# A chunked RWKV-7 recurrence followed by a low-rank mixer: the order of the steps of a slot written out, the block-diagonal state by VectorE, the mixer's u on tokens in place

## The chip, the cores and the metric

The kernel runs on one core of a Trainium2 chip. The metric is the device time of one execution in microseconds (us). Names of engines are those of the profile: PE is TensorE (PEld its weight loads), DVE VectorE, ACT ScalarE, POOL GpSimd, SP the engine that issues the DMAs. "Granted clock" is the share of full speed that TensorE's throttle granted, as the profile records it.

## The reference, cut to what matters

```
for t in range(S):                       # B=4, H=8, S=768, D=40, all float32
    y[t]  = einsum('bhd,bhde->bhe', r[t], state)
    Sa    = einsum('bhde,bhe->bhd', state, a[t])
    state = state * w[t][:, :, None, :] - Sa (x) b[t] + v[t] (x) k[t]
x = y as (B, S, H*D) = (4, 768, 320)
h = (x.T @ U) @ V                        # over the sequence, rank 32
u = x + h.T
out = u + relu(u @ w_ch1) @ w_ch2        # 320 -> 1280 -> 320
```

## The kernel before, in words

**Recurrence.** The sequence is cut into 12 chunks of L = 64 tokens. Two batch entries stand in the two halves of the 128 partitions, so there are 24 units of work (2 pairs of batches by 12 chunks), each with 8 heads. A unit passes through four generators, which `yield` between steps:

- `prep_f` needs only w, a, b: transposes of w and a (`pw`, `pa`), the running product of w by a scan on DVE (`PF`), its transposes `pp` and `pq`, a reciprocal `ip` on DVE, `nBT` on POOL, its transpose `pb`, and the scores `pf`, which go through DRAM (`fd`) into `ln`.
- `substitute` inverts triangular 16 by 16 blocks for two units at a time, in 14 pairs of small products on POOL (tiles `tmp`, `ln`), and stores the result to DRAM (`TD`), from where `fetch` reads it as `tc`.
- `prep_s` joins the blocks (`pg`, `g`, `px`, `t`, `pg2`, `GX`, `px2`), transposes v, r, k (`pv`, `pr`, `pk`) and makes the masked scores `e` and `cm` (from `pe`).
- `carry` is the part that depends on the unit before: `ph` from the state `ST`, `pX`, the outputs `py`, the transpose `pn`, the scores `pg` masked to `ng`, the gains `pd`, the new state `sn`, `sc`, `ST`, and `pS`, transposes of the state for the next unit's `py`. `ST` holds the state of a head pair as a block-diagonal matrix. `XTM` (tokens by 320, in SBUF) takes y.

In slot n stand `carry` of unit n, `prep_s` of unit n + 1, `prep_f` of unit n + 5 and, in every second slot, `substitute`. `merged` takes the step that is next by its share of its generator's steps. A tile framework then places every instruction on its engine's queue and may let it pass others; each engine works through its queue in order. The weights arrive as 64-bit floats in 27 pieces: `piece` loads one into `raw` and converts it to float32 by ACT, four DVE and four POOL instructions, one or two steps a slot.

**Mixer.** After a check of the inputs (`flag`, a branch) the second stage has 6 groups of 4 chunks (512 tokens). `mix(g)` makes `uf`, u transposed (features by tokens), in 3 tiles: transposes of `XTM` and on top of them, in the same PSUM bank, the low-rank part from `V_` and `hut`. `up_proj` makes `hid` in 5 pairs of PSUM banks (`p1`), one of each pair put out by ACT, one by DVE. `down_proj` sums 10 products in a bank, adds the low-rank part again on tokens, adds `XTM` and stores. The mixer's PSUM: 2 banks `p1`, 2 `pu`, 2 `p2`, 2 `ph`.

Of the kernel before, what the change touches and what calls it, by code (L numbers as in the profile page):

```python
# [37 lines left out]
def kernel(  # L38
# [85 lines left out]
    def piece(pool, dst, srcs):  # L124
# [10 lines left out]
        raw = pool.tile([128, WP, 2], I32, name="raw", bufs=2)  # L135
# [30 lines left out]
    with ExitStack() as p1:  # L166
# [106 lines left out]
        def prep_f(u):  # L273
# [17 lines left out]
            square(u, "A", u.nat["A"][:, :, 0:D], 1 / X_HI)  # L291
            yield
            p = one("pp")
# [9 lines left out]
            u.fa = hp.tile([128, NH, L], F32, name="fa")  # L303
            nc.vector.tensor_tensor(out=u.fa[:].rearrange("p h t -> p (h t)"), in0=pa[:], in1=pf[:, 0:NH * L],
                                    op=ALU.mult)
            nc.vector.tensor_copy(u.fa[:, :, 0:1], heads(pa[:])[:, :, 0:1])
            u.fa = u.fa[:].rearrange("p (i x) t -> p i (x t)", x=2)
            u.pe = hp.tile([128, NH, 1], F32, name="pe")
            nc.gpsimd.tensor_copy(u.pe[:], heads(pf[:, 1:])[:, :, L - 1:])
            yield  # L310
            bt = u.nat["BT"]
            nc.gpsimd.tensor_tensor(out=bt[:, :, 0:D], in0=u.nat["B"][:], in1=u.ip[:], op=ALU.mult)  # L312
            square(u, "B", u.nat["B"][:], 1 / X_HI)
            yield
# [3 lines left out]
            fb = qp.tile([128, NP, 128], F32, name="fb", tag="tr", bufs=2)  # L318
# [50 lines left out]
        def prep_s(u):  # L369
# [11 lines left out]
            fv = qp.tile([128, NP, 128], F32, name="fv", tag="tr", bufs=2)  # L381
# [4 lines left out]
            nc.scalar.activation(out=u.fr[:].rearrange("p i t -> p (i t)"), in_=pr[:], func=ACTF.Copy)  # L386
            pk = one("pk")
            up(kt, pk)
            fk = qp.tile([128, NP, 128], F32, name="fk", tag="tr", bufs=2)
            nc.scalar.activation(out=fk[:].rearrange("p i t -> p (i t)"), in_=pk[:], func=ACTF.Copy)  # L390
            square(u, "V", u.nat["V"][:, :, 0:D], 1 / X_HI)
            yield
# [11 lines left out]
            square(u, "R", u.nat["R"][:, :, 0:D], 1 / X_HI)  # L404
            yield
            p = two("pe")
            scores(p, fk, u.fa)
            scores(p, fv, u.fr, NP * DP)
            u.e = qp.tile([128, 2, NP, DP], F32, name="e", bufs=2)

            masked(u.e[:], p[:, :, 0:NP * DP])
            u.cm = qp.tile([128, 2, NP, DP], F32, name="cm", bufs=2)
            masked(u.cm[:], p[:, :, NP * DP:])
            square(u, "K", u.nat["K"][:], 1 / X_HI)
# [129 lines left out]
        def merged(*steps):  # L544

            lists = [[g, 0, n] for g, n in steps]
            while lists:
                x = min(lists, key=lambda x: (x[1] + 0.5) / x[2])
                if next(x[0], x) is x:
                    lists.remove(x)  # L550
                x[1] += 1

        wload = weights(wp)
        units = [Unit(n) for n in range(N)]
        AH = 5
# [235 lines left out]
```

## Time and profile before

| | before |
|---|---|
| median of 3 runs | 1073.66 us (1063.0 to 1081.65) |
| the profiled execution | 1072.85 us, of which the span of its instructions is 1071.0 us |
| PE busy | 903.6 us (84%) |
| DVE, ACT, POOL busy | 330.3, 251.7, 300.4 us |
| granted clock, mean | 0.835 |
| recurrence | first instruction to 707 us; first `XTM` write at 95.5 us, last at 705.2 us |
| mixer | 711.2 us to the end |

A PE matmul row counts records: a float32 matmul leaves two, a transpose one. "[0.80 <-DVE ng]" behind a row is idle time of the engine ahead of it and who ended it. Rows of the windows view give, for each engine, busy us and number of instructions, then the granted clock.

### The profile page before, as it was taken

The numbers are of one execution on the slowest core, as the hardware profiler recorded it, in microseconds if no ns is written. First come the engines' busy times: TensorE is split into PE (matmuls) and PEld (weight loads), VectorE is DVE, ScalarE is ACT, GpSimd is POOL, SyncE is SP. The second block draws the span as 40 slices with busy tenths as digits, with TensorE's granted clock in tenths as the row PEclk, the third lists the DMA queues.
The fourth block names the chain that finished last, engine by engine and source line by source line (L and its number), as shares of the span: only waits on it lengthen the run. The fifth ranks groups of instructions, "written<-read, shape, count | busy, mean of one in ns | idle before, by whom it ended". The sixth has DMA issues, their size and how long they took to land. (4 is left out here: it accounts for less than half of the span.)

```text
span 1071.0 us, 33742 instructions
## 1 busy us (share of the span) xinstructions
PE 903.6 (84%) x15146; PEld 675.0 (63%) x15146; DVE 330.3 (31%) x668; ACT 251.7 (23%) x630; POOL 300.4 (28%) x616
## 2 busy tenths in 40 slices
PE   2558789888788888888997868978989999999988
PEld 2447688777677787776886857853636455454635
DVE  5534334354434445443434214111111110101010
ACT  1223333333433343333333323200000000000010
POOL 5434524453625353525244446000000000000000
PEclk9656777787868787867779668669999999999999
DMA  4464342535252525443525221000000001010001
GB/s 97 70 96 80 50 85 42 95 48 99 45 99 45 96 48 99 70 73 51 94 42 91 51 61 27 3 3 0 13 13 13 12 1 25 1 24 1 22 3 25
DMA packets 262500, 51.19 MB, mean 48 GB/s; under 512 B 256112, under 2 KB 259216, under 8 KB 262352
## 3 DMA queue, kind: packets, MB, share of 16 engines
q1 hardware_dynamic: 262352, 49.01, 26.4%
q8 instruction: 119, 1.95, 0.7%
q14 instruction: 29, 0.24, 0.1%
HBM read 36.11 MB, written 12.86 MB: 46 GB/s over the span
## 5 line engine op out<-in xcount | busy, mean ns | idle before, releaser
L744 PE MATMUL p<-W,hid 128*128 128x320 f32 x480 | 135.8, 438 | 0.0
L729 PE MATMUL p<-uf,W 128*128 128x512 f32 x240 | 111.0, 605 | 16.6 <-ACT hid L734 16.6
L744 PEld LDWEIGHTS p<-W,hid 128*128 128x128 f32 x480 | 89.2, 190 | 45.3 <-issue 11.3
L729 PEld LDWEIGHTS p<-uf,W 128*128 128x128 f32 x240 | 43.1, 189 | 82.3 <-issue 45.8
L734 ACT ACTIVATE hid<-p 128x512 f32<-128x512 f32 x30 | 17.9, 597 | 324.1 <-PE p L732 324.1
L537 PE MATMUL pS<-ID,ST 128*128 128x128 f32 x176 | 43.9, 419 | 35.0 <-POOL ST L523 35.0
L296 DVE RECIPROCAL ip<-pp 128x320 f32<-128x320 f32 x24 | 51.8, 2158 | 46.1 <-PE pp L258 46.0
L735 DVE TENSOR_SCALAR hid<-p 128x512 f32<-128x512 f32 x30 | 20.8, 692 | 139.4 <-PE p L732 139.4
L537 PEld LDWEIGHTS pS<-ID,ST 128*128 128x128 f32 x176 | 35.2, 221 | 37.1 <-POOL ST L523 36.8
L436 PE MATMUL pg<-tt,fm 32*64 32x32 f32 x768 | 43.1, 277 | 13.1 <-DVE tt L428 11.6
L751 DVE TENSOR_TENSOR o<-p,XTM 128x320 f32<-128x320 f32 x24 | 11.8, 492 | 136.8 <-PE p L748 136.8
L436 PEld LDWEIGHTS pg<-tt,fm 32*64 32x64 f32 x768 | 40.0, 203 | 17.5 <-PE px L420 8.1
L156 POOL TENSOR_TENSOR low<-low,unit 128x320 f32<-128x320 f32 (+3 forms) x27 | 22.4, 829 | 100.9 <-ACT low L149 75.9
L350 POOL TENSOR_TENSOR ln<-ln,tmp 128x14 f32<-128x14 f32 (+6 forms) x168 | 45.4, 271 | 11.9
L348 POOL TENSOR_TENSOR tmp<-ln 128x14 f32<-128x14 f32 (+6 forms) x168 | 44.7, 266 | 12.7
L150 DVE TENSOR_SCALAR bits<-raw 128x320 int32<-128x320 int32 (+3 forms) x27 | 17.1, 634 | 96.4 <-DMA raw<-in_moe_w_ch_dram 75.2
L287 DVE COPY seg<-pw 128x8 f32<-128x8 f32 x24 | 4.1, 171 | 132.5 <-PE pw L253 132.5
L523 POOL TENSOR_TENSOR ST<-sc,slot 128x640 f32<-128x640 f32 x22 | 27.6, 1255 | 57.8 <-DVE sc L520 57.8
L446 PEld LDWEIGHTS px<-t,GX 32*64 32x64 f32 x768 | 39.3, 194 | 7.0 <-issue 4.8
L446 PE MATMUL px<-t,GX 32*64 32x32 f32 x768 | 43.7, 271 | 0.0
L312 POOL TENSOR_TENSOR nBT<-nB,ip 128x320 f32<-128x320 f32 x24 | 20.7, 863 | 77.3 <-DVE ip L296 72.4
L463 PE MATMUL ph<-nV,e 64*64 64x40 f32 x768 | 41.1, 282 | 0.0
(155 smaller groups left out, 1660.6 us busy)
## 6 DMA issues: line engine op xcount, KB each, us to landing
fd<-fn SPq DMA_DIRECT2D x48, 128.0 KB, 2.6
raw<-in_moe_w_ch_dram SPq DMA_DIRECT2D x18, 320.0 KB, 4.0
nW<-in_w_dram SPq DMA_DIRECT2D x48, 80.0 KB, 3.1
nA<-in_a_dram SPq DMA_DIRECT2D x48, 80.0 KB, 3.0
nB<-in_b_dram SPq DMA_DIRECT2D x48, 80.0 KB, 2.9
nR<-in_r_dram SPq DMA_DIRECT2D x48, 80.0 KB, 2.8
nK<-in_k_dram SPq DMA_DIRECT2D x48, 80.0 KB, 3.2
nV<-in_v_dram SPq DMA_DIRECT2D x48, 80.0 KB, 3.2
```

Of the source, the lines that this page charges most:

```text
L156: nc.gpsimd.tensor_tensor(out=g, in0=g, in1=e.bitcast(F32), op=ALU.mult)
L296: nc.vector.reciprocal(out=u.ip[:], in_=heads(p[:])[:, :, 0:D])
L348: nc.gpsimd.tensor_tensor(out=x, in0=ln[:, 0:j, j:j + 1].to_broadcast([128, j, n]), in1=ln[:, j:j + 1, j + 1:].to_broadcast([128, j, n]), ...
L350: nc.gpsimd.tensor_tensor(out=ln[:, 0:j, j + 1:], in0=ln[:, 0:j, j + 1:], in1=x, op=ALU.add)
L436: nc.tensor.matmul(out=pg[half(x), 32 * h:32 * h + 32], lhsT=fm[s, h, :], rhs=tt[s, h, :], start=True, stop=True)
L446: nc.tensor.matmul(out=px[half(x), 32 * h:32 * h + 32], lhsT=GX[s, h, :], rhs=t2[s, h, :], start=True, stop=True)
L463: nc.tensor.matmul(out=ph[half(x), s, i], lhsT=u.e[half(x), s, i, :], rhs=vt[half(x), 2 * i + s, 0:D], start=i + s == 0, stop=first, skip_ ...
L523: nc.gpsimd.tensor_tensor(out=ST[:, :, :, 0:D], in0=sc[:].rearrange("p i x e -> p (i x) e").unsqueeze(2).to_broadcast([128, NH, 2, D]), in ...
L537: nc.tensor.transpose(out=p[:, h // 4, 128 * (h % 4):128 * (h % 4 + 1)], in_=ST[:, h].rearrange("p s e -> p (s e)"), identity=ID[:])
L729: nc.tensor.matmul(out=ps_[x][:], lhsT=W1[i][:, (j + x) * 128:(j + x + 1) * 128], rhs=uf[i][:], start=(i == 0), stop=False)
L735: nc.vector.tensor_scalar_max(hid[:, j + 1, :], ps_[1][:], 0.0)
L744: nc.tensor.matmul(out=p[:, 0:DM], lhsT=hid[:, f, 2 * j * L:2 * (j + 1) * L], rhs=W2[:, f, :], start=(f == 0), stop=False, skip_group_chec ...
```

## The change

Five things.

1. `merged` goes; every slot runs the steps in one written order. `prep_f` has five steps instead of six, and its first one runs at the end of the slot before; there is one more slot at the beginning.
2. `ST` is written by DVE, in two `scalar_tensor_tensor` straight from `sn`; `sc` moves from DVE to POOL.
3. `carry` makes `pn` after its first `py`, and the gains are cut in two steps; the squares (a check of input ranges, on ACT) stand at other steps; the tiles `fb`, `fv`, `fk` have 3 buffers for 2.
4. `raw` has 1 buffer for 2, and a piece is loaded and converted within one slot's order.
5. The mixer adds the low-rank part once, on tokens and in place in `XTM` (`mix`), and transposes afterwards (`turn`). `hut` works in four column groups of PE and sums them by a matmul. `p1` has 4 banks, everything else in the mixer shares 2 (`pm`) and 2 (`p2`).

```
-        raw = pool.tile([128, WP, 2], I32, name="raw", bufs=2)
+        raw = pool.tile([128, WP, 2], I32, name="raw")
...
-                state["C"] = sc = qp.tile([128, NP, 2, D], F32, name="sc")
-                nc.vector.tensor_tensor(out=sc[:]..., in0=sn[:]..., in1=u.pe[:].to_broadcast([128, NH, D]), op=ALU.mult)
-                nc.gpsimd.tensor_tensor(out=ST[:, :, :, 0:D], in0=sc[:]..., in1=slot[:]..., op=ALU.mult)
+                sn = sn[:].rearrange("p i x e -> p (i x) e")
+                pe = u.pe[:].to_broadcast([128, NH, D])
+                for s in range(2):
+                    nc.vector.scalar_tensor_tensor(out=ST[:, :, s, 0:D], in0=sn, scalar=slot[:, s:s + 1], in1=pe,
+                                                   op0=ALU.mult, op1=ALU.mult)
+                state["C"] = sc = qp.tile([128, NP, 2, D], F32, name="sc")
+                nc.gpsimd.tensor_tensor(out=sc[:].rearrange("p i x e -> p (i x) e"), in0=sn, in1=pe, op=ALU.mult)
...
+        ORDER = "s c f l s c l c f c l s s l c c f l c s l w f s c l s f s l w"
...
-            merged(*gens)
-            next(wload, None)
-            if n >= 0:
-                next(wload, None)
+            fs = [units[x] if 0 <= x < N else None for x in (n + AH, n + AH + 1)]
+            for key in ORDER.split():
+                g = {"c": c, "s": s, "l": l}.get(key)
+                if key == "f":
+                    nf += 1
+                    x = fs[nf // 5]
+                    g = gen_f(x) if x else None
+                if key == "w" and n >= 1 - AH:
+                    g = wload
+                if g:
+                    next(g, None)
...
+    def hut(pr):
+        hs = mb.tile([128, 2, DM], F32, name="hs", bufs=1)
+        ps_ = [mps.tile([128, 512], F32, name=f"ph{x}", tag="pm", bufs=2) for x in range(2)]
+        for c in range(NCH):
+            for x in range(2):
+                nc.tensor.matmul(out=ps_[x][32 * (c % 4):32 * (c % 4) + 32, 0:DM], lhsT=U_[half(x), c, :],
+                                 rhs=XTM[half(x), pr * NCH + c, :], start=c < 4, stop=c >= NCH - 4,
+                                 skip_group_check=True)
+        nc.vector.tensor_copy(hs[:, 0, :], ps_[0][:, 0:DM])
+        nc.scalar.activation(out=hs[:, 1, :], in_=ps_[1][:, 0:DM], func=ACTF.Copy)
+        huts[pr] = t = mb.tile([RANK, 2, DM], F32, name="hut")
+        for x in range(2):
+            p = mps.tile([128, 512], F32, name="pq", tag="pm", bufs=2)
+            nc.tensor.matmul(out=p[0:RANK, 0:DM], lhsT=IB[:], rhs=hs[:, x, :], start=True, stop=True)
+            nc.vector.tensor_copy(t[:, x, :], p[0:RANK, 0:DM])
...
     def mix(g):
+        for c in range(th * GC, (th + 1) * GC):
+            p = mps.tile([128, 512], F32, name="pv", tag="pm", bufs=2)
+            for x in range(2):
+                nc.tensor.matmul(out=p[half(x), 0:DM], lhsT=V_[:, c * L:(c + 1) * L], rhs=huts[pr][:, x, :],
+                                 start=True, stop=True)
+            x = XTM[:, pr * NCH + c, :]
+            nc.vector.tensor_tensor(out=x, in0=p[:, 0:DM], in1=x, op=ALU.add)
...
-            for x in range(2):
-                nc.tensor.matmul(out=p[:].rearrange("p (j x t) -> p j x t", x=2, t=L)[:, :, x, :],
-                                 lhsT=huts[pr][:, x, 128 * i:128 * i + 128],
-                                 rhs=V_[:, th * GN:(th + 1) * GN], start=False, stop=x == 1,
-                                 skip_group_check=True)
...
-            ps_ = [mps.tile([128, 512], F32, name="p1") for _ in range(2)]
+            ps_ = [mps.tile([128, 512], F32, name="p1", bufs=4) for _ in range(2)]
...
-            for x in range(2):
-                nc.tensor.matmul(out=p[half(x), 0:DM], lhsT=V_[:, c * L:(c + 1) * L], rhs=huts[pr][:, x, 0:DM],
-                                 start=False, stop=True, skip_group_check=True)
...
+        up_proj(hid, uf, (0, 2))
+        if (g + 1) % NT == 0 and g + 1 < NG:
+            hut((g + 1) // NT)
+        up_proj(hid, uf, (4,))
+        if g + 1 < NG:
+            mix(g + 1)
+        up_proj(hid, uf, (6, 8))
+        if g + 1 < NG:
+            uf = turn(g + 1)
         down_proj(g, hid)
```

On PE, the second half of a slot of the recurrence before (from the scores `pg` of `carry` to the next unit's `ph`; L398, L420, L436 and L446 are the four steps that join the blocks in `prep_s`):

```order
L264 MATMUL pg<-fr,xf 64x64 x16
L264 MATMUL pe<-fa,fk 64x64 x16
L509 MATMUL pd<-nV_157,nKT_139 64x40 x16
L528 MATMUL py<-nBT_151,ng 64x40 x8
L398 MATMUL pg<-tt,fm 32x32 x32
L258 MATMUL pn<-ID,xf 128x128 x4
L420 MATMUL px<-tc,g 32x32 x11
L509 MATMUL pd<-nx,nBT_151 64x40 x16
L537 MATMUL pS<-ID,ST 128x128 x2
L436 MATMUL pg_5433<-tt,fm 64x32 x16
L446 MATMUL px_5504<-t_5398,GX 64x32 x6
L463 MATMUL ph<-nV_159,e 64x40 x16
```

The same stretch now (line numbers of the changed kernel: L399, L410, L434, L443 are the four joining steps):

```order
L264 MATMUL pg<-fr,xf 64x64 x16
L507 MATMUL pd<-nV_157,nKT_137 64x40 x16
L507 MATMUL pd<-nx,nBT_145 64x40 x16
L532 MATMUL py<-nBT_145,ng 64x40 x16
L399 MATMUL pg<-tt,fm 32x32 x32
L410 MATMUL px<-tc,g 32x32 x32
L264 MATMUL pf<-fa,fb 64x64 x16
L264 MATMUL pe<-fa,fk 64x64 x16
L541 MATMUL pS<-ID,ST 128x128 x8
L434 MATMUL pg_4102<-tt,fm 64x32 x16
L443 MATMUL px_4136<-t_4020,GX 64x32 x16
L460 MATMUL ph<-nV_159,e 64x40 x16
```

Between each of the four joining steps there now stands other work, the gains stand together, and `pS` stands five groups behind them. (Groups between these that did not change their place, as `pb`, `pw` and `pa`, are left out.)

On DVE, the end of `carry` and the start of the joining before (`tt<-tc` is the transposed block that L398 reads, `g` what L420 reads):

```order
L269 TENSOR_TENSOR ng<-pg,MU 128x512
L269 TENSOR_TENSOR cm<-pe,MU 128x512
L377 STREAM_TRANSPOSE tt<-tc 128x256
L530 SCALAR_TENSOR_TENSOR XTM,SQ<-py,qt 128x320
L402 TENSOR_TENSOR g<-pg,IB 128x256
L518 TENSOR_TENSOR sn<-pd,sc 128x320
L520 TENSOR_TENSOR sc<-sn,pe 128x320
```

And now:

```order
L269 TENSOR_TENSOR ng<-pg,MU 128x512
L521 TENSOR_TENSOR sn<-pd,sc 128x320
L525 SCALAR_TENSOR_TENSOR ST<-sn,slot,pe 128x8x40 x2
L376 STREAM_TRANSPOSE tt<-tc 128x256
L534 SCALAR_TENSOR_TENSOR XTM,SQ<-py,qt 128x320
L403 TENSOR_TENSOR g<-pg,IB 128x256
L418 STREAM_TRANSPOSE tt<-t_4955 128x256
L269 TENSOR_TENSOR e<-pe,MU 128x512
```

The new state and the two writes of `ST` now stand ahead of the transpose `tt<-tc`. Its place differs from slot to slot: of the 23 slots that have it, it is last behind `ST` and `XTM` in 5, behind two of the three in 6, between the two writes of `ST` in 3, directly behind `sn` in 4 and ahead of `ng` in 5.

On PE in the mixer, the end of one group's up projection and what follows before (p_11908 and p_11909 are the last pair of banks):

```order
L732 MATMUL p_11909<-uf_11797,W_2_92 128x512
L707 MATMUL pu<-ID,XTM 128x128 x4
L714 MATMUL pu<-V__89,hut 128x4x64 x2
L711 MATMUL pu<-ID,XTM 64x128 x8
L744 MATMUL p_11949<-W_93,hid 128x320 x10
L748 MATMUL p_11949<-hut,V__89 64x320 x2
```

And now, from the last matmul of the third pair (p_11780, p_11781):

```order
L751 MATMUL p_11781<-uf_11757,W_2_92 128x512
L717 MATMUL pv<-hut,V__89 64x320 x4
L748 MATMUL p_11806<-uf_11739,W_0_90 128x512
L731 MATMUL pu<-ID,XTM 128x128 x8
L762 MATMUL p_11851<-W_93,hid 128x320 x2
L734 MATMUL pu<-ID,XTM 64x128 x8
L762 MATMUL p_11866<-W_93,hid 128x320 x10
```

The low-rank products stand once, inside the up projection, and the transposes alone stand between the two projections.

More of the change, by code (lines that the diff above doesn't have):

```diff
@@ L503, in carry, with gains @@
             yield
[L504 to L511 removed]
+            p = two("pd")
+            def gains(y, z, start):
+                for i in range(NP):
+                    for x, s in ((0, 0), (1, 1), (0, 1), (1, 0)):
+                        nc.tensor.matmul(out=p[half(s), x, D * i:D * (i + 1)], lhsT=y[half(x), 2 * i + s, :],
+                                         rhs=z[half(x), 2 * i + s, 0:D], start=start and i == 0, stop=not start,
+                                         skip_group_check=True)
+            if not last:
+                gains(kt, vt, True)
+            yield
+            if not last:
+                gains(bt, nx, False)
                 dn = p[:, :, 0:NP * D].rearrange("p x (i e) -> p i x e", e=D)
```

127 lines of the change are left out of this document (49 added, 78 removed).

## The prediction

> **What bounds the kernel now.** First the windows view, cut at the first and the 21st write of `XTM` by `carry` and at the start of the mixer (columns: stretch, then busy us and instructions of PE, PEld, DVE, ACT, POOL, granted clock, DMA share, GB/s), with the two timeline rows that set the cuts.
>
> ```profile
> 0.00:95.50 95.50, 48.58 (x812) 41.53 (x812) 44.75 (x102) 26.99 (x70) 42.58 (x118) 0.75 0.51 87
> 95.50:645.40 549.90, 462.24 (x11752) 410.69 (x11753) 220.91 (x452) 191.19 (x495) 240.24 (x481) 0.76 0.40 69
> 645.40:707.00 61.60, 53.83 (x1338) 48.66 (x1336) 17.49 (x40) 15.58 (x35) 17.61 (x18) 0.70 0.04 10
> 711.20:1071.00 359.80, 338.95 (x1248) 174.14 (x1248) 47.03 (x76) 17.92 (x30) 0.00 (x0) 0.99 0.05 11
> 95.53 0.49 DVE L530 SCALAR_TENSOR_TENSOR XTM<-py,qt 128x320 f32<-128x320 f32 x1 [0.51 <-PE py L528]
> 645.39 0.45 DVE L530 SCALAR_TENSOR_TENSOR XTM<-py,qt 128x320 f32<-128x320 f32 x1
> ```
>
> PE carries both stages: 84% busy in the 20 full slots, 94% in the mixer; no other engine passes 44% there. A slot takes 549.9 / 20 = 27.5 us, of which PE idles 87.7 / 20 = 4.4 us. And PE runs at a mean clock of 0.76. Single windows show only 1.00 and 0.50 (a 0.99 is a cut beside the window's edge), so it is at half speed for 48% of the time. Next, who is waited for (PE's waits in these 20 slots: us in total, times, longest), and what the clock does, in windows of 3.4 us.
>
> ```profile
> PE pS L537 <- POOL ST L523: 34.6, 10, 9.1
> PE pd L509 <- DVE ng L269: 12.2, 16, 0.8
> PE pg L436 <- DVE tt L428: 10.6, 10, 1.2
> ```
>
> ```profile
> 284.10:287.50 3.40, 2.13 (x116) 1.84 (x107) 2.99 (x5) 0.00 (x0) 2.34 (x7) 1.00 0.70 109
> 287.50:290.90 3.40, 2.71 (x128) 2.25 (x127) 1.19 (x3) 0.44 (x1) 2.69 (x10) 1.00 0.12 22
> 325.00:328.40 3.40, 3.40 (x28) 3.01 (x30) 0.58 (x2) 1.89 (x7) 1.27 (x1) 0.50 0.00 0
> 328.40:331.80 3.40, 3.40 (x113) 3.15 (x113) 0.00 (x0) 2.73 (x8) 0.59 (x1) 0.99 0.14 25
> 366.00:369.40 3.40, 2.29 (x107) 1.95 (x103) 3.07 (x7) 0.00 (x0) 0.86 (x1) 1.00 0.62 104
> 369.40:372.80 3.40, 3.40 (x112) 2.84 (x112) 0.42 (x1) 0.44 (x1) 0.86 (x1) 0.50 0.65 145
> ```
>
> A window at full clock with 1.27 us idle stayed at 1.00 (first pair), one with 1.11 us idle fell to 0.50 (last pair): about 1.2 us of idle PE in one window is the point where it tips. The middle pair is a return to full clock: that window holds `pb` and `pS`, twelve transposes without a gap. So every short wait is paid twice, once itself and once as a spell at half clock.
>
> What the work of a slot costs at full clock, from the PE timeline:
>
> ```profile
> 303.38 1.93 PE L463 MATMUL ph<-nV,e 64*64 64x40 f32 x32
> 305.24 1.33 PE L468 MATMUL ph<-ST,fa 128*64 128x80 f32 x16
> ...
> 323.69 1.92 PE L436 MATMUL pg<-tt,fm 32*64 32x32 f32 x32 [1.06 <-DVE tt L428]
> ...
> 328.29 0.74 PE L264 MATMUL pf<-fa,fb 64*64 64x64 f32 x32
> 330.01 1.13 PE L463 MATMUL ph<-nV,e 64*64 64x40 f32 x32
> 331.07 0.77 PE L468 MATMUL ph<-ST,fa 128*64 128x80 f32 x16
> 340.14 0.68 PE L509 MATMUL pd<-nV,nKT 64*64 64x40 f32 x32 [0.80 <-DVE ng L269]
> 344.24 0.55 PE L509 MATMUL pd<-nx,nBT 64*64 64x40 f32 x20 [0.68 <-issue]
> 345.21 0.54 PE L528 MATMUL py<-nBT,ng 64*64 64x40 f32 x10
> ```
>
> The same `ph` took 305.24 - 303.38 = 1.86 us at half clock and 331.07 - 330.01 = 1.06 us at full: a factor of 1.75, so a spell at half clock loses 43% of its length. One slot's work runs from L436 at 323.69 to the end of `py` at 345.75: 4.6 us at half clock (to 328.29), worth 2.6 at full, and 17.46 - 0.80 - 0.68 = 16.0 us at full. Together **18.6 us a slot**. The other 27.5 - 18.6 - 4.4 = 4.5 us are the loss to half clock.
>
> **The change, recurrence.** No matmul is removed there, so the 18.6 us stay; what can go are 4.4 us of gaps and 4.5 us of clock.
>
> Gaps that go. `ST` leaves POOL, where it cost 1.26 us in a queue that also holds the block inversion:
>
> ```profile
> L523 POOL TENSOR_TENSOR ST<-sc,slot 128x640 f32<-128x640 f32 x22 | 27.6, 1255 | 57.8 <-DVE sc L520 57.8
> 344.82 0.49 DVE L518 TENSOR_TENSOR sn<-pd,sc 128x320 f32<-128x320 f32 x1 [2.40 <-PE pd L509]
> 345.42 0.49 DVE L520 TENSOR_TENSOR sc<-sn,pe 128x320 f32<-128x320 f32 x1
> 345.83 0.49 DVE L530 SCALAR_TENSOR_TENSOR XTM<-py,qt 128x320 f32<-128x320 f32 x1
> 317.20 0.49 DVE L530 SCALAR_TENSOR_TENSOR XTM<-py,qt 128x320 f32<-128x320 f32 x1 [0.51 <-PE py L528]
> 317.62 0.44 DVE L377 STREAM_TRANSPOSE tt<-tc 128x256 f32<-128x256 f32 x1
> 318.21 1.08 PE L398 MATMUL pg<-tt,fm 32*32 32x32 f32 x64 [1.05 <-DVE tt L377]
> ```
>
> Each of the two new DVE writes is taken at 0.49 us, the row of the same size and kind (`XTM`); bounds are half of it and POOL's 1.26. `pS` now stands five groups (`pb`, `px`, `pf`, twice `pe`) behind the gains, so its 34.6 us go. The gains now have `pk` ahead of them and `ng` is read only by `py` behind them (12.2 us go); the joining steps have `pb`, then `pf`, `pe`, `pS`, then `pw`, `pa` between them (10.6 us and the waits on issue go). `sc` costs POOL about 0.86 us beside PE, less than the 1.26 it gives up. The squares and the third `tr` buffer are costed at nothing: ACT is busy 191 of 550 us; in a slot where a square stands just ahead of `GX` or `nx` it is 0.65 us, which I put into the unforeseen part below.
>
> A gap that stays or grows: L399 (L398 before) waits for `tt<-tc`, which shares DVE with `sn`, the two `ST` and `XTM`. With all four ahead, by the rows: 0.03 to `sn`, 0.60 to the first `ST` (345.42 - 344.82), 0.41 to the second (345.83 - 345.42), 0.41 to `XTM`, 0.42 to the transpose (317.62 - 317.20), 0.44 for it and 0.15 to PE: 2.46 us after the gains. PE has only `py` to do meanwhile, 1.06 us as `ph` of the same shape: **1.40 us idle**. Behind three of them 0.98, between the `ST` 0.57, behind `sn` 0.15, else none. With 5, 6, 3, 4 and 5 such slots that is 15 us; waiting for `g` behind `pb` alone adds some 0.2 us a slot. Sum 0.9 us a slot, and 0.6 for what I cannot foresee: 1.5.
>
> Clock. A 1.40 us gap falls into one window of 3.4 us with at least 1.2 us about 7 times in 10, a 0.98 us gap with the 0.2 of `g` perhaps 3 in 10: 5 x 0.7 + 6 x 0.3 = 5 spells in 23 slots. Each should last until `pf`, `pe`, `pS` have filled a window; before, from L398 at 318.21 to `pf` at 328.29, such a spell took 10 us, about 9 of them work: 4 us lost. That is 21 us; doubled for unforeseen gaps, 1.9 us a slot.
>
> New slot: 18.6 + 1.5 + 1.9 = 22.0 us, **5.5 us less, 110 us over 20 slots**. The last three slots (59.8 us) have fewer steps; at some 15% less, 9 us. The first 95.5 us are left as they are: the same steps of `prep_f` stand there one behind the other. Recurrence: **-119 us**.
>
> Does another engine take over at 22 us? DVE needs 221 / 20 = 11.0 plus 0.5, POOL 12.0, ACT 9.6: on average no. POOL in a slot with the inversion has some 16 us, still less.
>
> The 325.00 row holds mostly transposes, and the clock rose behind it; so I let a spell end at `pS`. The Trainium skill, "TensorE: Matmul & The Clock Gate" ("Part 4: PE-mode transpose"), says instead that a transpose does not count as activity of PE in the same way; by that rule the spells would last past `pS`, about twice as long, and the sum would be 42 us higher, 962. The row does not agree with it.
>
> **The change, mixer.**
>
> ```profile
> PE p L729 <- ACT hid L734: 16.6, 24, 0.8
> 781.36 3.70 PE L729 MATMUL p<-uf,W 128*128 128x512 f32 x8
> 838.23 1.98 PE L729 MATMUL p<-uf,W 128*128 128x512 f32 x4
> L744 PE MATMUL p<-W,hid 128*128 128x320 f32 x480 | 135.8, 438 | 0.0
> L714 PE MATMUL pu<-V__89,hut 32*128 32x256 f32 x72 | 19.7, 397 | 0.0
> L748 PE MATMUL p<-hut,V__89 32*64 32x320 f32 x96 | 18.1, 453 | 0.0
> L695 PE MATMUL ph<-XTM,U__88 64*32 64x320 f32 x96 | 14.7, 464 | 4.3 <-SPq L604 4.3
> ```
>
> A group took 838.23 - 781.36 = 56.9 us, on PE alone and at full clock. Four `p1` banks give PE a free pair while the last is put out: -16.6 us. The low-rank part inside the transposed tiles (L714) goes: -19.7. The one on tokens (L748) only moves, and its 24 adds of 0.49 us lie on DVE, busy 13% there. `hut` is bounded by its 14.7 us and a quarter of that (four column groups). L748, which uses two column groups, took 18.1 / 96 = 0.19 us a record, L744 of the same length 0.28, so I take 9. Its summing matmuls (4 records x 0.28), two copies that PE waits for, and a first `mix` with nothing beside it cost 8 back. Sum: -16.6 - 19.7 - 5.7 + 8 = **-34 us**, between -28 and -40.
>
> **Sum.** 1072.85 - 119 - 34 = 920 us against the profiled execution, which lies 0.8 us under the median of the runs.
>
> **The rivals.**
>
> *The clock holds.* If the gaps are split by the windows' edges, or shorter than worked out, none tips a window: slots of 18.6 + 1.5 = 20.1 us, 148 us less in 20 slots, and 9 + 34: 882 us. The Trainium skill, "TensorE: Matmul & The Clock Gate" ("Why this matters for your kernels"), asks only that no idle gap between matmuls exceeds some 3 us; by that rule no spell would be left and these 882 us would come out. The trace does not agree: at 366.00, 1.11 us in one window was enough.
>
> *A spell in every slot, as before.* If two small gaps meet in most windows, 4.5 us of clock loss stay, with 2.5 us of gaps: slots of 25.6, 38 us less, and 5 + 34: 996 us. For it: a PE that runs faster makes every hand-over to DVE or ACT relatively later.
>
> *The order does not take.* The framework still moves instructions past each other (L399 is written ahead of the gains and stands behind `py`). If the waits only change names, the mixer alone is left: 1039 us.
>
> *Slower: the single `raw` buffer.*
>
> ```profile
> DVE bits L150 <- DMA raw<-in_moe_w_ch_dram: 75.2, 11, 14.7
> raw<-in_moe_w_ch_dram SPq DMA_DIRECT2D x18, 320.0 KB, 4.0
> ```
>
> DVE waited 75.2 / 11 = 6.8 us for `raw` in half of the slots, hidden by its slack. Now L150 stands between `cm` and the scan, with the scan, `fa` and `ip` queued behind it and PE's `pp` behind those, some 1 us of cover. If the load, which can only start when the last conversion has read the buffer, lands 6.8 us late in all 22 slots, that is 22 x (5.8 + 4 of clock) = 216 us on top: 1136 us. It decides from 5 us of lateness a slot. Against it: a load takes 4.0 us to land and now has most of a slot.
>
> **Chances.** Forecast 0.55, clock holds 0.15, a spell in every slot 0.20, order does not take 0.06, slower 0.04. The range 875 to 1000 holds the first three but for their edges. A measurement of this kernel tells about 2% from no change: faster 0.93, same 0.04, slower 0.03.
>
> **What would show it.** Right: mean clock in the slots above 0.85, slots near 22 us, no PE wait for `ST`, the wait for `tt<-tc` the largest left, and about 51 us a mixer group without gaps. Wrong: PE waiting for DVE's scan or for `raw`, a clock still near 0.76, or slots whose idle time exceeds 2 us.

## The result, and the profile after

The changed kernel takes 920.25 us (median of 4 runs, 911.8 to 929.0) against 1073.85 us (median of 4): a ratio of 0.853, 95% interval 0.841 to 0.866. This ratio and those below compare only executions in the faster of two states, for the change those of 911.8 and 914.5 us; medians are of all executions. The profiled execution took 911.8 us, its span 910.1 us at a mean granted clock of 0.902.

The windows view after, cut at the same places as before: the first and the 21st write of `XTM`, then the last slots, then the mixer (columns: stretch, busy us and instructions of PE, PEld, DVE, ACT, POOL, granted clock, DMA share, GB/s).

```profile
0.00:89.70 89.70, 46.41 (x784) 38.46 (x784) 48.85 (x107) 28.82 (x74) 46.95 (x123) 0.79 0.54 93
89.70:535.80 446.10, 391.33 (x11728) 350.24 (x11732) 237.85 (x468) 193.55 (x491) 231.95 (x480) 0.88 0.50 85
535.80:592.40 56.60, 49.04 (x1401) 43.90 (x1390) 17.55 (x41) 15.92 (x36) 12.05 (x13) 0.79 0.04 11
596.60:910.10 313.50, 308.08 (x1184) 161.90 (x1184) 54.95 (x96) 22.41 (x38) 0.00 (x0) 0.99 0.05 13
```

Read against the rows of before, the 160.9 us of span are: 5.8 at the start (95.5 to 89.7), **103.8 in the 20 full slots** (549.9 to 446.1), 5.0 from there to the mixer's first matmul (711.2 - 645.4 against 596.6 - 535.8), **46.3 in the mixer** (359.8 to 313.5). A slot went from 27.5 to 22.3 us. PE's idle time there (stretch less busy) went from 87.7 to 54.8 us, the clock from 0.76 to 0.88. Who PE waits for in those 20 slots (us in total, times, longest):

```profile
PE pg L399 <- DVE tt L376: 23.1, 14, 3.0
PE pe L264 <- issue: 12.1, 8, 2.4
PE px L410 <- issue: 7.0, 10, 1.7
PE pf L264 <- issue: 6.2, 5, 2.0
PE pS L541 <- issue: 2.0, 3, 1.1
```

and two rows of the same view of before that the prediction did not show:

```profile
PE px L420 <- issue: 10.1, 8, 2.1
PE pg L398 <- DVE tt L377: 4.2, 4, 1.1
```

`ST` (34.6 us before), `ng` (12.2) and `tt<-t` (10.6) are gone. The wait for `tt<-tc` has grown from 4.2 to 23.1 us; that it grows was forecast. The next three rows (25.3 us; before, `px` and `pe` had 11.5) were not forecast: here PE waits for nothing that the profile names.

**What "issue" is here.** The PE timeline shows that these gaps lie inside a group of equal matmuls, where no operand is new:

```profile
248.38 0.49 PE L264 MATMUL pf<-fa,fb 64*64 64x64 f32 x8
250.83 0.91 PE L264 MATMUL pf<-fa,fb 64*64 64x64 f32 x22 [1.96 <-issue]
```

The DMA view, cut to 248.30 to 248.50 and to 248.50 to 248.70, has no packet of queue q8 in the first and one in the second. The row of the second:

```profile
q8 instruction: 1, 0.02, 27.5%
```

and that of the whole page (packets, MB, share of 16 engines):

```profile
q8 instruction: 119, 1.95, 0.8%
```

1.95 MB in 119 packets are 16 KB each, and PE's 15082 matmul and 15082 load records make 253 to a packet, so I take q8 for PE's instruction stream; the run with px in halves, below, bears this out. PE stops at 248.87, a packet starts between 248.5 and 248.7, PE goes on at 250.83. Over the traces of nine kernels of this study, 148 stops of over 0.8 us lie inside a group in the 20 slots; 136 of them end 2.0 to 2.8 us behind the start of an instruction packet, the other 12 within 3.2. Of the 92 such gaps between two groups, which have other causes, 17 do. The stops come where small matmuls are densest: `pg` (L399), `px`, `pf`, `pe`, some 450 records (matmuls and loads) in about 4 us of work. The Trainium skill, "Runtime: NRT & Kernel Launch" ("Instruction fetch mechanics"), calls the crossing of such a 16 KiB block mostly hidden. Here it is not: these three rows are 25 us of 446.

**The clock** falls by the same kind of window as before. Three windows of 3.4 us around that stop, on the throttle's own edges:

```profile
244.42:247.83 3.41, 2.11 (x118) 1.72 (x115) 2.25 (x7) 0.26 (x1) 2.78 (x9) 1.00 0.77 133
247.83:251.25 3.42, 1.46 (x74) 1.29 (x64) 0.45 (x1) 1.09 (x3) 2.87 (x10) 0.50 0.18 67
251.25:254.66 3.41, 3.41 (x89) 3.29 (x82) 1.15 (x2) 2.44 (x8) 0.35 (x1) 0.50 0.28 49
```

1.30 us idle in the first (the wait for `tt<-tc`): the second is at 0.50. The third has no gap and holds six of the transposes `pS`: the clock is full from 254.66 on. In the 20 slots there are 16 spells of 6.6 us on average, 106 us in all; before there were 20 of 13.0 us, 259 us. The change made the spells shorter more than rarer.

**The mixer** by groups:

```profile
L762 PE MATMUL p<-W,hid 128*128 128x320 f32 x480 | 131.6, 434 | 0.0
L748 PE MATMUL p<-uf,W 128*128 128x512 f32 x240 | 112.5, 608 | 0.0
L717 PE MATMUL pv<-hut,V__89 32*64 32x320 f32 x96 | 16.0, 440 | 0.1
L700 PE MATMUL ph<-XTM,U__88 64*32 64x320 f32 x96 | 5.0, 563 | 4.1 <-SPq L610 4.1
L708 PE MATMUL pq<-hs,IB 128*32 128x320 f32 x8 | 2.5, 434 | 0.8 <-ACT hs L704 0.8
```

The wait of the up projection (16.6 us) is gone, the low-rank part in the transposed tiles (19.7) too, `hut` fell from 14.7 to 5.0, its summing costs 2.5 + 0.8. The down projection fell from 135.8 to 131.6 although its matmuls are the same, and the low-rank part on tokens from 18.1 to 16.0. Of the rows shown only L748 rose, from 111.0 to 112.5.

### The profile page after: what moved, and what is told of

It is laid out like the page before. It is cut to its first block, busy times and chain, and to the rows that moved or that the text cites. A ratio compares the mean times of both kernels' runs of the same rounds, so it can differ in the third digit from the quotient of the medians.

```text
span 910.1 us, 33712 instructions
## 1 busy us (share of the span) xinstructions
PE 795.0 (87%) x15082; PEld 594.5 (65%) x15082; DVE 359.3 (39%) x710; ACT 260.7 (29%) x638; POOL 290.9 (32%) x616
## 3 DMA queue, kind: packets, MB, share of 16 engines
q8 instruction: 119, 1.95, 0.8%
## 5 line engine op out<-in xcount | busy, mean ns | idle before, releaser
L762 PE MATMUL p<-W,hid 128*128 128x320 f32 x480 | 131.6, 434 | 0.0
L748 PE MATMUL p<-uf,W 128*128 128x512 f32 x240 | 112.5, 608 | 0.0
L748 PEld LDWEIGHTS p<-uf,W 128*128 128x128 f32 x240 | 43.2, 190 | 61.1 <-issue 58.4
L754 DVE TENSOR_SCALAR hid<-p 128x512 f32<-128x512 f32 x30 | 20.8, 692 | 116.8 <-PE p L751 116.8
L373 POOL TENSOR_TENSOR fm<-fn,MF 128x512 f32<-128x512 f32 x24 | 30.5, 1269 | 107.3 <-PE pg L434 107.3
L300 DVE RECIPROCAL ip<-pp 128x320 f32<-128x320 f32 x24 | 51.8, 2157 | 21.6 <-PE pp L258 21.5
L399 PE MATMUL pg<-tt,fm 32*32 32x32 f32 x1536 | 19.7, 201 | 32.5 <-DVE tt L376 29.8
L269 DVE TENSOR_TENSOR ng<-pg,MU 128x512 f32<-128x512 f32 x24 | 16.6, 692 | 75.0 <-PE pg L264 75.0
L318 ACT ACTIVATE fb<-pb 128x512 f32<-128x512 f32 x24 | 14.3, 597 | 91.5 <-PE pb L253 91.5
L399 PEld LDWEIGHTS pg<-tt,fm 32*32 32x32 f32 x1536 | 17.3, 112 | 35.5 <-issue 19.3
L269 DVE TENSOR_TENSOR e<-pe,MU 128x512 f32<-128x512 f32 x24 | 16.6, 691 | 45.7 <-PE pe L264 45.7
L751 PE MATMUL p<-uf,W 64*128 64x512 f32 x120 | 33.9, 641 | 0.0
L541 PE MATMUL pS<-ID,ST 128*128 128x128 f32 x176 | 31.7, 334 | 2.0 <-issue 2.0
L434 PEld LDWEIGHTS pg<-tt,fm 32*64 32x64 f32 x768 | 28.0, 149 | 6.5 <-DVE size L155 1.7
L443 PE MATMUL px<-t,GX 32*64 32x32 f32 x768 | 29.4, 228 | 2.6 <-ACT GX L436 2.6
L434 PE MATMUL pg<-tt,fm 32*64 32x32 f32 x768 | 31.0, 232 | 0.8 <-issue 0.7
L253 PE MATMUL pw<-ID,nWC 128*128 128x128 f32 x96 | 18.8, 328 | 14.6 <-DVE nWC L279 14.6
```

Source lines behind the costliest of these rows:

```text
L269: nc.vector.tensor_tensor(out=o, in0=x.rearrange("p s (i t) -> p s i t", t=DP), in1=MU[:].unsqueeze(1).unsqueeze(1).to_broadcast([128, 2, ...
L300: nc.vector.reciprocal(out=u.ip[:], in_=heads(p[:])[:, :, 0:D])
L373: nc.gpsimd.tensor_tensor(out=fm[:], in0=u.fn[:].rearrange("p s (i t) -> p (s i) t", t=DP), in1=MF[:].unsqueeze(1).to_broadcast([128, NH, ...
L399: nc.tensor.matmul(out=pg[s, 32 * h:32 * h + 32], lhsT=fm[s, h, 32 * (q % 2):32 * (q % 2) + 32], rhs=tt[s, h, :], start=True, stop=True)
L434: nc.tensor.matmul(out=pg[half(x), 32 * h:32 * h + 32], lhsT=fm[s, h, :], rhs=tt[s, h, :], start=True, stop=True)
L443: nc.tensor.matmul(out=px[half(x), 32 * h:32 * h + 32], lhsT=GX[s, h, :], rhs=t2[s, h, :], start=True, stop=True)
```

## The experiments

The theory after the result: (a) the order of the steps, not the engine that writes `ST`, makes the gain of the recurrence; (b) the mixer stands by itself; (c) what is left in a slot is the wait for `tt<-tc` and PE's own instruction stream, and each costs clock besides. Rivals: `ST` on VectorE carries the gain; the "issue" gaps are waits for a bank or a copy that the profile fails to name. Where runs are compared in us, the difference is that of their ratios, times 1073.85 us. The table gives for the 20 full slots the length of one, the clock, PE's idle time and the sum of the issue waits of `px`, `pf` and `pe`.

| run | median us | slot us | clock | idle us | issue us |
|---|---|---|---|---|---|
| before | 1073.85 | 27.5 | 0.76 | 87.7 | 11.5 |
| mixer alone (the slots are those of before) | 1023.9 | 26.9 | 0.78 | 86.9 | 11.0 |
| the change | 920.25 | 22.3 | 0.88 | 54.8 | 25.3 |
| two banks for p1 (the slots are those of the change) | 940.7 | 23.0 | 0.85 | 55.7 | 22.8 |
| hut in one column group (the same) | 926.75 | 23.3 | 0.84 | 56.5 | 25.2 |
| ST by VectorE in the old order | 1063.3 | 26.9 | 0.75 | 61.7 | 11.5 |
| ST by GpSimd in the new order | 923.1 | 22.9 | 0.87 | 58.4 | 29.9 |
| early tc | 910.7 | 21.9 | 0.91 | 49.6 | 24.9 |
| pS ahead of pf | 919.4 | 22.8 | 0.88 | 61.0 | 28.4 |
| early tc, pS ahead of pf | 884.4 | 21.1 | 0.95 | 42.2 | 14.5 |
| px in halves | 1001.7 | 25.0 | 0.81 | 66.5 | 45.2 |
| early tc, pS ahead, pv first | 892.5 | 20.8 | 0.94 | 37.0 | 18.7 |
| early tc, pS behind pf, pv first | 884.7 | 21.1 | 0.94 | 42.1 | 21.6 |
| eight transposes added behind px | 905.2 | 21.8 | 0.95 | 46.3 | 20.6 |

Three rows have the slots of the change, untouched: idle time and issue waits repeat within 2.5 us, but the clock does not, and a slot takes 22.3 to 23.3 us, shortest in the profiled execution of the change. The two rows with the slots of before differ by 0.6. So a slot that is less than 1 us shorter or longer tells nothing by itself.

**The mixer alone.** The recurrence of before with `hut`, `mix`, `turn`, `up_proj` and `down_proj` of the change.

> The recurrence of before (merged order, ST by GpSimd, two raw buffers) with the mixer of the change. By the prediction's sum the mixer alone is worth 34 us (28 to 40): 1040 us. By the trace of the changed kernel, whose mixer took 313.5 us against 359.8, it is worth 46 us: 1027 us, and its groups show no idle TensorE. If a part of the gain came from the recurrence handing over differently, the mixer here takes more than 320 us.

Measured: 1023.94 us, ratio 0.961 (0.951 to 0.971).

```profile
701.00:1017.10 316.10, 311.15 (x1184) 163.44 (x1184) 54.92 (x96) 22.40 (x38) 0.00 (x0) 0.98 0.05 13
```

The mixer took 316 us, 44 less than before, and under 320: it stands by itself. The prediction's 34 us were too few.

**ST by VectorE in the old order.** Before, with this edit alone:

```
-                nc.vector.tensor_tensor(out=sc, in0=sn, in1=pe, op=ALU.mult)
-                nc.gpsimd.tensor_tensor(out=ST[:, :, :, 0:D], in0=sc, in1=slot, op=ALU.mult)
+                for s in range(2):
+                    nc.vector.scalar_tensor_tensor(out=ST[:, :, s, 0:D], in0=sn, scalar=slot[:, s:s + 1], in1=pe, ...)
+                nc.gpsimd.tensor_tensor(out=sc, in0=sn, in1=pe, op=ALU.mult)
```

> Before, with one part of the change: the two ST writes by VectorE and sc by GpSimd, everything else in the old merged order. If the order carries the gain of the recurrence (my theory), this takes only part of the 34.6 us wait of pS for ST: pS still stands right behind py, and sn and two ST writes of 0.5 us against 1.06 us of py leave some 0.5 us a slot; gaps fall by about 25 us and the clock a little: 1035 to 1050 us. If the move of ST off GpSimd is the main thing, most of the 115 us come already here: about 970 us.

Measured: 1063.3 us, ratio 0.993 (0.988 to 0.999), less than I expected of it.

```profile
PE pS L538 <- DVE ST L522: 18.0, 14, 2.4
```

The wait for `ST` halves (34.6 to 18.0), PE's idle time falls by 26 us, yet the 20 slots take 538.1 us, as long as the same slots with `ST` by GpSimd in the run with the mixer alone (538.7), for the clock is at 0.75: there are 22 spells of 12.6 us. Idle time taken away where others remain in the same windows paid little here, some 7 us by the ratio.

**ST by GpSimd in the new order.** The changed kernel with the reverse of that edit.

> The changed kernel with ST back on GpSimd (sc on VectorE, one ST write of 1.26 us behind it). In the new order pS stands five groups behind the gains, about 6 us; theory: pS waits 1 to 2 us in the slots with a block inversion on GpSimd and not in the others: 10 to 25 us more, 930 to 945 us. Rival: ST on VectorE is what makes the order work; then the wait of 34 us comes back with its clock loss, 960 us or more.

Measured: 923.12 us, ratio 0.864 (0.856 to 0.872) where the change has 0.853 (0.841 to 0.866): no difference that can be told. The 960 us of the rival did not come; the expected 10 to 25 us more are 12 by the ratios, inside the intervals.

```profile
PE pS L540 <- POOL ST L526: 3.3, 4, 1.7
```

Five groups between the gains and `pS` hide `ST` on either engine, but for 3.3 us. With the run before, this shows (a) as far as the engine goes: the second of the five edits gives nothing that could be told here once the order is written out. What else changed in the recurrence (the gains cut in two, the third buffers, the single `raw` buffer) was not tried apart from the order.

**Early tc.** The load of `tc` for the next slot's `prep_s` stands at the head of a slot instead of at its end:

```
-            if 0 <= n + 2 < N:
-                fetch(units[n + 2])
...
+            if 0 <= n + 2 < N:            # ahead of the loop over the steps
+                fetch(units[n + 2])
             nf = 0
             for key in ORDER.split():
```

> The changed kernel with the load of tc issued at the start of a slot and not at the end of the slot before its use, so that VectorE transposes it directly behind ng, ahead of sn and both ST writes. The wait of L399 for tt<-tc (23.1 us in 14 slots of the 20) goes. If each of these gaps also brings a spell at half clock, about 8 of them at some 2 us of loss: 20 us more, about 880 us, with the clock in the slots at 0.92 or above. Rival: TensorE then reaches the end of its fetched instructions earlier, and the gaps that start within 2 us of an instruction packet (32 us in the 20 slots) grow by what was saved: 905 to 915 us.

Measured: 910.69 us, ratio 0.851 (0.843 to 0.860): the change's own within the uncertainty.

```profile
PE pg L264 <- ACT xf L477: 12.9, 18, 0.7
PE pe L264 <- issue: 10.5, 6, 2.7
```

The wait for `tt<-tc` is gone from the list, but the framework, which places instructions by its own estimate of when data is there, now puts `pg<-xf` directly behind `pX`: 18 waits of 0.7 us for the copy `xf`. The time lies in the rival's range, and the 880 us were missed, but the issue waits did not grow (24.9 us), so the rival's reason, that they take back what was saved, is wrong too. Half of the gap went into a new wait.

**pS ahead of pf.** One letter of the written order moves:

```
-        ORDER = "s c f l s c l c f c l s s l c c f l c s l w f s c l s f s l w"
+        ORDER = "s c f l s c l c f c l s s l c c f l c s c l w f s l s f s l w"
```

> The changed kernel with the eight transposes pS moved ahead of pf and pe, directly behind px (one letter of the written order). Theory: the gaps of TensorE named issue in pf and pe are waits for its own instructions, since each ends 2.1 to 2.7 us behind the start of an instruction packet and lies in the stretch L399, px, pf, pe, where 64 to 224 small matmuls run in 4 us. Sixteen slow instructions (1 us) in that stretch give the fetch 1 us more: the waits in pf and pe fall from 21 us by some 13, with a few spells less: 900 to 910 us. Rival: these gaps are waits for a bank or a copy that the profile does not name; then they stay in pf and pe at 21 us, and 920 us stay, or more where pS now waits for ST.

Measured: 919.42 us, ratio 0.855 (0.845 to 0.865): nothing gained.

```profile
PE pS L541 <- DVE ST L525: 21.3, 17, 2.1
PE pe L264 <- issue: 14.3, 8, 3.0
```

Now the distance that hid `ST` is too short: 21.3 us of waiting for it, and `pf` and `pe` still wait 21.2 us on issue, where the fetch theory had expected some 8. This is what the rival forecast. By the trace, for six of the eight stops at `pe` the instruction packet starts only in `pe` itself, behind `pS`, where a spacer ahead of it comes too early; why it starts so late here, and for no stop at `pe` with both edits below, is open.

**Both edits.**

> Both edits together: tc loaded at the start of the slot, and pS ahead of pf and pe. If the fetch theory holds and what the early tc gave was taken back by fetch waits, the two gains add or do better: 890 to 900 us. If pS as a spacer does nothing, 910 us as with the early tc alone.

Measured: 884.42 us, ratio 0.827 (0.821 to 0.832), 29 us under the change by the ratios, where the two alone gave 2 and nothing.

```profile
PE pg L264 <- ACT xf L477: 12.9, 18, 0.7
PE px L410 <- issue: 6.9, 8, 1.2
PE pe L264 <- issue: 5.3, 8, 1.2
PE pS L541 <- DVE ST L525: 3.8, 4, 1.3
```

`tt<-tc` no longer stands behind `ST`, and `ST` is mostly ready when `pS` comes (3.8 us of waiting for 21.3). Against early tc alone, from which only the place of `pS` differs, the issue waits of `pf` and `pe`, behind `pS`, fall from 17.3 to 7.6 us, those of `px`, ahead of it, stay (7.6 and 6.9), and the half-speed time falls from 79 to 44 us (7 spells). So here `pS` works as a spacer, as it did not in the run before. This version beats both kernels.

**Two banks for p1.**

```
-            ps_ = [mps.tile([128, 512], F32, name="p1", bufs=4) for _ in range(2)]
+            ps_ = [mps.tile([128, 512], F32, name="p1", bufs=2) for _ in range(2)]
```

> The changed kernel with two p1 banks in the up projection, not four. The prediction's term: the wait of L748 for the copies comes back, 16.6 us in 24 waits of 0.7 us: 937 us. Rival: the new order of mix and turn between the pieces of the up projection covers part of it: under 930 us.

Measured: 940.72 us, ratio 0.875 (0.866 to 0.884), 23 us over the change by the ratios.

```profile
PE p L748 <- ACT hid L753: 12.7, 18, 1.0
```

```profile
614.40:940.80 326.40, 308.19 (x1184) 161.09 (x1184) 54.93 (x96) 22.39 (x38) 0.00 (x0) 0.99 0.05 13
```

In the mixer itself it is 12.9 us (326.4 against 313.5), 18 waits and not 24: the new order covers six of them, as the rival said, though its 930 us did not come. The rest lies in the recurrence, which this edit does not touch: the 20 slots took 459.5 us for 446.1, and its first matmul of the mixer came at 614.4 us in this profiled execution, at 596.6 in that of the change, which was the fastest of its four.

**hut in one column group.**

```
-                nc.tensor.matmul(out=ps_[x][32 * (c % 4):32 * (c % 4) + 32, 0:DM], ..., start=c < 4, stop=c >= NCH - 4, ...)
+                nc.tensor.matmul(out=ps_[x][0:RANK, 0:DM], ..., start=c == 0, stop=c == NCH - 1, ...)
```

> The changed kernel with hut in one column group as before (no summing matmuls, no copies to sum). Prediction's terms: hut in four groups saves 5.7 us and its summing costs part of 8 us, so that the two about cancel: 918 to 922 us. By the trace of the changed kernel hut took 5.0 us against 14.6 and the summing 2.4 + 0.8: 926 us.

Measured: 926.75 us, ratio 0.858 (0.850 to 0.866). The medians cannot tell 6 us; its mixer can.

```profile
616.20:938.80 322.60, 317.73 (x1176) 166.70 (x1176) 53.80 (x94) 21.52 (x36) 0.00 (x0) 0.98 0.05 13
```

```profile
L699 PE MATMUL ph<-XTM,U__88 64*32 64x320 f32 x96 | 16.0, 495 | 4.0 <-DVEq L610 4.0
```

322.6 against 313.5: the four column groups are worth 9 us, 11.0 in `hut` itself (16.0 to 5.0) less 3.3 for their summing, and the rest elsewhere.

**px in halves.** The same products, in twice as many instructions, in the dense stretch:

```
-                    nc.tensor.matmul(out=px[s, 32 * h:32 * h + 32], lhsT=g[s, h, :], rhs=u.tc[s, h, :], ...)
+                    for e in (0, 16):
+                        nc.tensor.matmul(out=px[s, 32 * h + e:32 * h + e + 16], lhsT=g[s, h, :], rhs=u.tc[s, h, e:e + 16], ...)
```

> The changed kernel with each 32-column matmul of px issued as two of 16 columns: the same result, 64 matmuls and 64 weight loads more in each slot, in the stretch where TensorE stops. Work alone: 64 records at the 11.6 ns that a px record takes at full clock are 0.74 us a slot, 17 us in all: 937 us, with the issue gaps of px, pf and pe at 28 us as before. If TensorE waits there for its instructions, half a packet of 256 more in that stretch costs about half of the 2.3 us that a packet takes: 1.2 us a slot more, 23 us of gaps and some 10 us of clock on top: 960 to 970 us, and these gaps above 45 us.

Measured: 1001.65 us (988.05 to 1013.16), some 80 us over the change (its two shortest, 988 and 994 us, against 911.8 and 914.5), more than the theory's 40 to 50.

```profile
PE px L411 <- issue: 22.9, 17, 2.8
PE pe L264 <- issue: 12.6, 12, 2.4
PE pf L264 <- issue: 9.7, 5, 2.3
q8 instruction: 131, 2.15, 0.9%
```

The last row is that of queue q8 for the whole page: 3072 records more (1536 matmuls, 1536 loads) are 12 packets more, 256 to a packet, so q8 carries PE's instructions. The issue waits went from 25.3 to 45.2 us, with no operand, bank or copy added: with the times of the packets, this shows that PE waits for its instructions, and the rival, an unnamed bank or copy, falls, in spite of the run with `pS` ahead. The time is larger than that: of 54.7 us more in the 20 slots, idle time is 11.7 (66.5 - 54.8; the wait for `tt<-tc` fell to 16.4), 15 are the new records at 11.6 ns, and 25 are clock, 0.81 for 0.88 (59 us more of PE's work ran at half speed, at a loss of 43%); 3 stay open. What I had allowed for clock was 10.

**pv first, in two versions.** Both with early tc, and with `pv` and `pr` written ahead of `ph`, so that `py` stands behind `pX`; `pS` ahead of `pf` in one, behind it in the other.

```
+        ORDER = "t s s c f l c l c f c l s s l c c f l c s c l w f s l s f s l w"     # t: fetch
+        ORDER = "t s s c f l c l c f c l s s l c c f l c s l w f c s l s f s l w"
```

> Early tc and pS ahead of pf as in the run with both, and pv and pr written ahead of ph, so that py, and no longer pg, stands behind pX. The wait of pg for xf (12.9 us in 18 slots) goes: at 0.7 us each it seldom tips the clock alone: 865 to 878 us. If pv and pr were what filled the stretch ahead of L399 and their place now lacks work, a wait for kt or tt comes in its place: 884 us or more.

> As the run with pv and pr first, but pS between pf and pe instead of ahead of pf. By the fetch theory a spacer is as good there for pe and not for px and pf, and the wait of pS for ST (3.8 us, up to 21 us where VectorE is late) goes: within 8 us of the other, with the issue gaps of pf higher and those of pe lower. If the spacer must come before the first stop (px), it is 10 us or more slower.

Measured: 892.47 us, ratio 0.839 (0.830 to 0.847), and 884.68 us, ratio 0.829 (0.822 to 0.835). The wait for `xf` went, as it should, and the slots of the first are the shortest in the table (20.8 us), yet neither beats the version with both edits.

```profile
PE px L410 <- issue: 11.1, 10, 2.5
```

```profile
PE px L410 <- issue: 9.9, 10, 1.7
PE pd L507 <- issue: 6.0, 6, 1.6
```

The first row is the largest wait of the first version; the other two, with 7.0 us at `pf` between them, are the largest of the second. With named waits nearly gone, what is left of them is PE's instruction stream, at `px` and now at `pd` too. The first expectation (865 to 878) was missed for that reason in part; its other case, a wait for `kt` or `tt`, did not come (0.4 us for `tt`), and the rest lies outside the slots and stays open. The second version lies within 8 us of the first, as expected, with higher issue waits at `pf` (7.0 for 2.3), but not lower ones at `pe` (4.4 for 4.3); that the spacer must come before the first stop is not borne out.

**A spacer behind px.** The changed kernel with eight transposes of the identity a slot, into columns that nothing reads:

```
+            for i in range(8):
+                nc.tensor.transpose(out=px[:, 256 + 128 * (i % 2):384 + 128 * (i % 2)], in_=ID[:], identity=ID[:])
```

> The changed kernel with eight transposes of the identity added behind px in each slot, into columns of px's bank that nothing reads. Their work: 1.0 us a slot, 23 us. If waits for instructions are what stops pf and pe (18 us), sixteen slow instructions ahead of them take most of that away, and if windows with many transposes raise the clock, the spells that begin at L399 end here and not at pS, 3 to 4 us sooner: half-speed time falls from a quarter of the slots to an eighth, worth 20 us or more: 895 to 910 us in all, the clock in the slots 0.92 or above. If transposes do not count as activity, the clock in the slots stays at 0.88 and only the instruction waits pay: about 930 us. If neither holds, 943 us.

Measured: 905.2 us, ratio 0.848 (0.840 to 0.857): some 23 us of work added, and 5 us less by the ratios, which the intervals do not tell from nothing. The work does not show in the time: the case of 943 us did not come.

```profile
90.60:526.60 436.00, 389.74 (x11880) 346.66 (x11880) 239.39 (x472) 190.01 (x491) 237.81 (x485) 0.95 0.52 88
```

```profile
PE px L445 <- ACT GX L438: 9.1, 2, 8.6
PE pe L264 <- issue: 9.0, 9, 2.0
PE pg L399 <- DVE tt L376: 8.4, 10, 2.6
PE pf L264 <- issue: 1.7, 2, 0.9
```

The waits of `pf` and `pe` fall from 18.3 to 10.7 us, and the half-speed time from 106 to 44 us. But not as I had put it: the 6 spells left are no shorter (7.4 us against 6.6), there are fewer. And the framework placed L399 otherwise beside them, so that its wait fell from 23.1 to 8.4 us; a single wait of 8.6 us for `GX` came anew. So this run shows that added work can pay for itself here; whether the transposes hold the clock up or only the smaller gaps do, it leaves open.

## Why the prediction came out right, and where it did so by luck

- **PE's gaps and the clock bound the recurrence: right.** The same matmuls took 103.8 us less in 20 slots (110 forecast).
- **"ST leaves POOL", a part of the reason given for the 34.6 us: wrong as a cause.** The wait went because the order puts five groups between the gains and `pS`; it goes with `ST` on either engine (3.3 us are left with POOL).
- **Gaps that stay, 1.5 us a slot: too few.** 54.8 / 20 = 2.7 us. The mechanism of the term for `tt<-tc` is as worked out, but the term was too small, 15 us for 23.1:

```profile
244.47 1.06 DVE L525 SCALAR_TENSOR_TENSOR ST<-sn,slot,pe 128x320 f32<-128x320 f32 x2
245.46 0.43 DVE L376 STREAM_TRANSPOSE tt<-tc 128x256 f32<-128x256 f32 x1
246.03 0.91 PE L399 MATMUL pg<-tt,fm 32*32 32x32 f32 x64 [1.30 <-DVE tt L376]
223.25 1.57 DVE L525 SCALAR_TENSOR_TENSOR ST<-sn,slot,pe 128x320 f32<-128x320 f32 x2
223.29 0.72 POOL L528 TENSOR_TENSOR sc<-sn,pe 128x320 f32<-128x320 f32 x1 [3.98 <-DVE sn L521]
225.32 0.74 PE L399 MATMUL pg<-tt,fm 32*32 32x32 f32 x64 [1.82 <-DVE tt L376]
```

  The prediction took each write of `ST` at 0.49 us. The last three rows, of another slot, show what it missed: there POOL makes `sc` from the same `sn` at the same time, and the two writes take 1.57 us and not 1.06. All 13 writes beside `sc` took 1.00 to 1.12 us, 29 with POOL idle or at its small products 0.50 to 0.61, and two beside `nKT` 0.54 and 1.14. Of the 14 waits for `tt<-tc`, the 9 behind such a write are 18.8 of the 23.1 us. So the term was mis-sized where `sc` on POOL meets the writes of `ST`; `sc` left on DVE behind them was not tried.

  The 0.6 us for the unforeseen had to hold the instruction stream, 25.3 / 20 = 1.3 us. The row was there before the change (`px` waited on issue, 10.1 us in 8), and I read it as one that the order would cure. Why it grew is open: the new order puts `pg`, `px`, `pf` and `pe` one behind the other, and a PE that waits less may reach the end of its instructions sooner, though with early tc it did not.
- **Clock, 1.9 us a slot: right in size by luck, and not in its parts.** Not ten spells with 4 us lost each, but 16 with 2.6: of PE's 391 us, 98 ran at half speed, and 43% of that is 42 us or 2.1 a slot. In the two other profiled executions of these slots the same sum gives 2.8 and 3.0.
- **Work, 18.6 us a slot: too much.** What is left of 22.3 - 2.7 - 2.1 is 17.5. This error of 1.1 hid that of the gaps. Part of it is that one slot stood for twenty: by the same sum all 20 slots of before have 18.2 us each (462.2 of PE's work, 229 of it at half speed). Why the same matmuls then took 0.7 us less is open.
- **The tipping point of about 1.2 us held, as a soft one.** In 13 traces, windows at full clock in the recurrence with 1.0 to 1.2 us idle stayed full 47 times in 64, with 1.2 to 1.6 us 44 in 111, with more 5 in 100. The rival "the clock holds", which the Trainium skill's bound of some 3 us of idle ("TensorE: Matmul & The Clock Gate", "Why this matters for your kernels") would have given, did not come.
- **Transposes and the clock: the row was right.** Of gap-free windows at half speed with 12 transposes or more, 59 of 61 were followed by full clock; with none or one, 18 of 125. The rule of the Trainium skill, "TensorE: Matmul & The Clock Gate" ("Part 4: PE-mode transpose"), by which a transpose does not count as activity in the same way, would have made it 962 us. But these windows were only observed: they also hold few of the small matmuls, and at the start of the mixer a window that held `hut` alone, without a transpose (596.0 to 599.4), was followed by full clock too.
- **The mixer, -34: mis-sized by 12.** Three terms: the 8 us that the summing matmuls, copies and the first `mix` should cost back were 3.3 (2.5 + 0.8); `hut` gained 9.7 and not 5.7; and the down projection lost 4.2 us that the sum had at nothing. Before, each of its chains of ten ended in matmuls of the low-rank part, with 32 rows and in two column groups; that these slowed the chains is my reading, not tried. The p1 term (16.6) was fully there in the trace; the run with two banks shows 12.9 of it as owed to the banks alone.
- **The start (0) and the last three slots (-9)** were -5.8 and -5.0. What shortened the start was not tried.
- **The rival with one raw buffer** did not come: DVE's wait for the weights fell from 75.2 us to

```profile
DVE bits L150 <- DMA raw<-in_moe_w_ch_dram: 7.8, 2, 7.1
```

  since a piece is now loaded at the end of a slot and converted in the next one (as one loaded at 245.9 us and converted from 254.7 on).

The medians differ by 153.6 us, the sum said 153; the profiled executions differ by 161. That the forecast came so near is luck: gaps and work were wrong by about 1 us a slot each and cancelled, and the recurrence's 119 us were 115 where the mixer's 34 were 46.

## What to carry to other kernels

Where the clock falls by idle time within a window of 3.4 us, count idle time by window and not by wait: 26 us less idle gave some 7 us where every slot kept its spell, 33 us less gave 104 us in the slots where the spells became half as long. Fix the order before moving work between engines, since enough distance between producer and consumer hides either. When named waits are gone, look at waits named issue inside groups of equal instructions: many small matmuls in a row outran their own instruction stream here, and slow instructions put between them (eight transposes that had to be done anyway, moved ahead) gave it time in one of two tries. When an operation moves to another engine, look at what then runs beside it: a write of `ST` took twice as long beside `sc` on POOL.

## What the runs showed of the hardware that was not expected

- PE's instructions come in 16 KB packets of 256 records (3072 records more were 12 packets more), and 136 of 148 stops inside a group ended 2.0 to 2.8 us behind a packet's start; doubling the records of one group added 20 us of such stops in 20 slots.
- Four column groups: the 96 records of the two `hut` took 5.0 us in four groups of 32 columns and 16.0 in one.
- A write of `ST` by VectorE took 1.00 to 1.12 us beside GpSimd's `sc`, which reads the same `sn`, and 0.50 to 0.61 with GpSimd idle or at its small products.
- Eight transposes added to each slot, some 23 us of work, did not make the kernel slower (ratio 0.848 against 0.853).
